# A unit's attention issued in fewer, longer TensorE steps, the state's update as two products of 64 columns, and x's remainder subtracted by VectorE

## The chip, the cores and the metric

The kernel runs on one core of one Trainium2 chip. The metric is the device time of one execution in microseconds (us). The engines are TensorE (PE in the profile; its weight loads have a row of their own, PEld), VectorE (DVE), ScalarE (ACT), GpSimd (POOL) and SyncE (SP), which issues the DMAs. All arithmetic is in 32-bit floats; "fp32" and "fp32r" below are two ways in which TensorE takes them.

## The reference

The program is a complex linear attention followed by a feed-forward layer. For every batch entry b (4) and head h (8) a complex state S of 48 x 48 is carried over 768 positions t; a is first scaled so that its magnitude is at most 0.999:

```
S_t = a_t * S_(t-1) + k_t v_t^T         (complex a_t along k's 48 channels, real k, v)
y_t = q_t^T Re(S_t)
x   = y as (4*768, 8*48) = (3072, 384)
out = gelu(x @ w_in) @ w_out            (384 -> 2048 -> 384)
```

## The kernel before, in words

**Lanes.** The recurrence is made parallel by cutting the 768 positions into chunks: four of 64 positions, then four of 128 (`GROUPS`; two chunks are a group). The running products of a are made on 128 lanes by VectorE, position by position (`scan`, L621), with ScalarE, GpSimd and TensorE helping before and after; k and q are multiplied by the products or their inverses and written to DRAM (`kq`). This is done group by group, lanes 0 to 3.

**Units.** A unit is one batch entry and 128 positions, 24 in all (`unit`, L737). It reads kqn (128 positions x 8 heads x 2 x 96: for each head k's 96 columns, then q's 96, real and imaginary part) and vn (8 heads x 64 columns, of which 48 are v). TensorE then makes, with fp32r transposes, k and q turned (`turn`, L819, four heads at a time); the scores of four heads (`scores`, L831, fp32, 96 rows x 128 columns); `y` (L843, fp32: 128 rows x 64 weight columns, two heads in the two halves of the columns); `y_state` (L849: what comes from the state, 96 rows x 48 columns, two heads side by side in the same way); and for the state's update `add_state` (L801) one fp32 product per head: weights k of 96 columns, moving v of 48. Units 0 to 7 hold two chunks of 64 positions each, units 8 to 23 one chunk of 128; the last chunk of each batch entry (units 20 to 23) needs no update. Between two chunks the state is turned (multiplied by a complex gain): in units 0 to 5 by two TensorE products with 96 weight columns (`turn_by_pe`, L787), from unit 6 on by VectorE or ScalarE and GpSimd (`turn_state`, L775).

**x and its remainder.** The feed-forward layer works with numbers split into an fp32r part (hi) and a remainder (lo). For x = y in PSUM, ScalarE writes hi in two pieces (128 x 128, called x, and 128 x 384, called xT) and sums them for a check of the input's range; TensorE then subtracts hi from y in PSUM with two fp32r products by minus the identity; ScalarE or VectorE copies what is left as lo; six DMAs place one piece (`xT<-x`).

**Blocks.** A block is two or three units' x, 256 or 384 columns (`block`, L913), nine blocks of 2, 3, 3, 3, 3, 3, 3, 2 and 2 units. For each of 16 slices of the middle layer TensorE does nine fp32r products (`first`), ScalarE gelu twice (gh, gf), VectorE or GpSimd gl = gf - gh, and TensorE nine (six) products for the output (`second`). A block needs the x of all of its units before its first product.

**Order.** All of this is written as steps to a list (`Plan`, L109). `either` and `both` leave a step's engine open. `together` makes several TensorE instructions one step, which is issued as a whole when all of its inputs are there. A list scheduler (`forward`, L267) with estimated costs (`FIXED`, `EACH`, `PASS`, `SWITCH`) simulates the engines and takes at each moment the ready step of highest rank; ranks come from the longest way to the end (`natural`) plus a constant for each kind of work (`MORE`). So the instructions' order on each engine is fixed before the run, and each engine works through it in order. A step with at most 64 weight columns in fp32 counts as "narrow", and a change between narrow and not narrow costs `SWITCH` in the estimate.

All instructions issued from the list show line 390 (or 388) in the profile, so they are told apart by their tiles. "att" is a ring of three PSUM banks for units, "ph" and "po" the banks of the blocks.

Of the kernel before, what the change touches and what calls it, by code (L numbers as in the profile page):

```python
# [10 lines left out]
F32 = mybir.dt.float32  # L11
F32R = mybir.dt.float32r
# [65 lines left out]
BYTES = 3.6e5  # L78

ROUND, PASS = 0.462e-3, 0.4219e-3  # L80
SWITCH = 0.09
STAY = 0.0
COLD, WARM = 3.0, 4.0
TABLES = {AF.Ln: "natural_log_exp_and_others", AF.Exp: "natural_log_exp_and_others", AF.Gelu: "gelu"}
NEAR = 0.076
# [5 lines left out]
N_A = 4  # L91
WL = 0.307

MORE = dict(lanes0=-11.06, lanes1=28.05, lanes2=-175.66, lanes3=359.97, weights=-54.39, units=96.75, blocks=41.59)
BIAS = dict(vector=0.49, scalar=-0.32, gpsimd=0.38)


class Step:


    def __init__(self):
        self.options, self.table, self.port = {}, None, set()
        self.before, self.after, self.chain, self.weight = set(), [], None, 1.0
        self.data, self.narrow = 0.0, False


class Plan:
# [16 lines left out]

    @contextmanager
    def together(self):
        self.open = []
        yield
        calls, self.open = self.open, None
        self.add(calls)  # L130
# [27 lines left out]
    def add(self, calls):  # L158
        step = Step()
        n = len(self.steps)  # L160
        engine = calls[0][0]
        cost = 0.08 * (engine == "scalar" and len(calls) > 1)
        for call in calls:
            outs, ins = self.operands(call)
            cost += self.cost(call, outs, ins)
            if engine == "tensor":
                step.narrow = call[1] == "matmul" and call[3]["rhs"].dtype != F32R and call[3]["lhsT"].shape[1] <= 64
            if engine == "sync":
                step.data = max(0.05, math.prod(c for _, c in outs[0].ap) * 4 / BYTES)
            for x in tuple(call[2]) + tuple(call[3].values()):  # L170
                step.table = TABLES.get(x, step.table) if isinstance(x, AF) else step.table
            for x, writes in [(x, False) for x in ins] + [(x, True) for x in outs]:
                self.hold(step, n, x, writes)
        step.options[engine] = calls, cost
        self.ports(step, engine, calls)
        step.before.discard(n)
        step.chain, step.weight = self.chain.get(engine, (None, 1.0))
        step.kind, step.part = self.kind, self.part
        self.steps.append(step)
# [87 lines left out]
    def forward(self, rank):  # L267
# [6 lines left out]
        free = dict.fromkeys(FIXED, 0.0)  # L274
        table = None
        channel = 0.0
        warm, narrow = 0.0, False
        port = dict.fromkeys(FIXED, 0.0)
        other = {"vector": "gpsimd", "gpsimd": "vector"}
        first = lambda some: max(some, key=lambda i: (rank[i], -i))  # L280
# [1 line left out]
        while len(order) < len(steps):  # L282
            best = None
            for e, waiting in pool.items():
                if not waiting:
                    continue
                t = max(free[e], min(ready[i] for i in waiting)) + NEAR
                fits = [i for i in waiting if ready[i] <= t]
                i = first(fits)
                if e == "tensor" and STAY and steps[i].narrow != narrow:  # L290
                    same = [j for j in fits if steps[j].narrow == narrow and rank[j] > rank[i] - STAY]
                    i = first(same) if same else i
                if len(steps[i].options) > 1:
                    ends = {o: max(free[o], ready[i], port[other[o]] if o in steps[i].port else 0.0) + c + BIAS[o] for o, (_, c) in steps[i].options.items()}
                    if ends[e] > min(ends.values()) + 1e-9:
                        fits = [i for i in fits if len(steps[i].options) == 1]
                        if not fits:
                            continue
                        i = first(fits)
                start = max(free[e], ready[i])  # L300
                if e in steps[i].port:
                    start = max(start, port[other[e]])
                if best is None or start < best[0]:
                    best = start, i, e
# [9 lines left out]
            if e == "tensor":  # L314
                if start - free[e] > COLD:
                    warm = start + WARM
                if start < warm:
                    cost *= 2
                cost += SWITCH * (s.narrow != narrow)
                narrow = s.narrow  # L320
            free[e] = end = start + cost
            if e in s.port:
                port[e] = end
# [77 lines left out]
def lanes_and_chunks(ctx, tc, flags, a_lanes, x_lanes, v_units, w_in, w_out, out):  # L401
# [25 lines left out]
    nc.gpsimd.memset(sj, -1.0)  # L427
    nc.gpsimd.affine_select(sj, sj, pattern=[[0, 1]], compare_op=ALU.is_gt, fill=1.0, base=D, channel_multiplier=-1)

    other_half = cst.tile([D2, D2], F32, name="other_half")  # L430
    nc.scalar.mul(other_half[:, 0:D], ident[0:D2, D:D2], -1.0)
    nc.scalar.mul(other_half[:, D:D2], ident[0:D2, 0:D], -1.0)

# [303 lines left out]
    def unit(u):  # L737
# [32 lines left out]
        def bank():  # L770

            p = next(ps_early if early else ps_att)
            return bank() if any(p is x for x in held) else p
# [13 lines left out]
        def turn_by_pe(i, b):  # L787

            sb = st[b]
            m2 = next(m2s)  # L790
            P.vector.tensor_tensor(out=m2.rearrange("p c (h e) -> p c h e", h=H), in0=vap(sb, [[0, 2], [D, H], [1, D]]),
                                   in1=vap(gain[i - 1][:, :, b * H:(b + 1) * H], [[BH, 2], [1, H], [0, D]]), op=ALU.mult)
            p = bank()[0:D2, 0:DM]
            with P.together():
                P.tensor.matmul(out=p, lhsT=ident[0:D2, 0:D2], rhs=m2[:, 0], start=True, stop=False)
                P.tensor.matmul(out=p, lhsT=other_half[:], rhs=m2[:, 1], start=False, stop=True)
            sf = sb.rearrange("p h e -> p (h e)")
            P.either(("scalar", "copy", (sf, p), {}), ("vector", "tensor_copy", (sf, p), {}))
            return p

        def add_state(chunk, turned):  # L801

            i, _, _, t0, size, b = chunk
            sf = st[b].rearrange("p h e -> p (h e)")
            p = bank()[0:D2, 0:DM] if turned is None else turned
            for hh in range(2):
                with P.together():
                    for h in range(hh * 4, hh * 4 + 4):
                        P.tensor.matmul(out=p[:, h * D:(h + 1) * D], lhsT=kn[t0:t0 + size, h], rhs=vn[t0:t0 + size, h, 0:D], start=turned is None, stop=True, skip_group_check=turned is not None)
            if turned is not None:  # L810
                P.either(("scalar", "copy", (sf, p), {}), ("vector", "tensor_copy", (sf, p), {}))
            elif i == 0:
                P.vector.tensor_copy(sf, p)
            else:
                P.vector.tensor_tensor(out=sf, in0=p, in1=sf, op=ALU.add)

        qT, kT, kp, pm = [], [], [], []

        def turn(src, dst, nm, hh):  # L819
            p = next(ps_att)  # L820
            with P.together():
                for j in range(4):
                    P.tensor.transpose(out=p[0:D2, j * 128:(j + 1) * 128].bitcast(F32R), in_=src[:, hh * 4 + j, :].bitcast(F32R), identity=ident_r[:])
            t = next(qTs if nm == "qT" else kps)
            src = p[0:D2, :].rearrange("p (j l) -> p j l", j=4)
            P.either(("scalar", "copy", (t[0:D2], src), {}), ("vector", "tensor_copy", (t[0:D2], src), {}))
            dst.append(t[0:D2])
            if nm == "kT":
                kp.append(t)

        def scores(hh):  # L831
            p = next(ps_att)
# [23 lines left out]
        if early:  # L856
# [4 lines left out]
            held.append(bank())  # L861
            py = held[0].rearrange("p (c l) -> p c l", c=4)
            for hh in range(2):
                turn(kn, kT, "kT", hh)
                turn(qn, qT, "qT", hh)
                scores(hh)
                y(hh)
                for c in with_state:
                    y_state(c, hh)
            for c in with_state:  # L870
                add_state(c, turned[c])
        else:
            for hh in range(2):
                turn(kn, kT, "kT", hh)
                turn(qn, qT, "qT", hh)
                scores(hh)
            held.append(bank())
            py = held[0].rearrange("p (c l) -> p c l", c=4)
            y(0)
            y(1)  # L880
            for c in chunks:
                turned = None
                if c[0]:
                    turned = (turn_by_pe if u < UPE else turn_state)(c[0], c[5])
                    y_state(c, 0)
                    y_state(c, 1)
                if c[0] < NP - 1:
                    add_state(c, turned)
        j = next(j for j in range(len(BLOCKS)) if u < first_unit[j + 1])
        if u == first_unit[j]:  # L890
            xblk[j] = next(xTs)
# [2 lines left out]
        parts = ((py[:, 3], x67[:, 0], x67[:, 1], fc), (py[:, 0:3], xt[:, :, 0], xt[:, :, 1], fc + 1))  # L894
        for at, hi, _, f in parts:
            P.scalar.activation(hi, at, AF.Copy, accum_out=flags[:, f:f + 1])
        with P.together():
            for at, hi, _, _ in parts:
                P.tensor.matmul(out=at, lhsT=minus[:], rhs=hi, start=False, stop=True, skip_group_check=True)
        for at, _, lo, _ in parts:  # L900
            P.either(("scalar", "copy", (lo, at), {}), ("vector", "tensor_copy", (lo, at), {}))

        for c in range(NCC):
            for p0 in (0, 64):
# [317 lines left out]
```

## Time and profile before

| | us |
|---|---|
| median of 3 runs (730.65 to 735.02) | 732.39 |
| the profiled execution's own time | 732.53 |
| its span, first to last instruction | 730.7 |
| PE busy / DVE busy / ACT busy / POOL busy | 672.6 / 452.2 / 457.0 / 72.6 |

A row of a timeline reads: start, duration (both us from the span's start), engine, line, operation, out<-in, shapes, and how many instructions were merged. A matmul's duration holds its way through the array, so successive ones overlap: what one costs is read from the start of one row to the start of the next. An fp32 matmul shows as two records (x8 for four heads). In "128*96 128x48" the first pair is the weights (rows x columns), the second the moving operand. PE's granted clock was 1.00 from 120 us on but for the very end.

### The profile page before, as it was taken

Reading aid. Unit: us, or ns where it says so; the run is one execution under the profiler, and the core shown is the slowest. Engines: PE = TensorE matmul, PEld = TensorE weight load, DVE = VectorE, ACT = ScalarE, POOL = GpSimd, SP = SyncE. Lnnn points to the kernel's source line nnn. Section 1 sums busy time; section 2 is a strip of 40 time slices with the busy share of each in tenths; the row PEclk is TensorE's granted clock in tenths of the full one; section 3 lists DMA queues with packets and bytes.
Section 4 is the critical chain, followed back from the end, with each engine's and each line's share of the span. In section 5 each row is a group of like instructions: output and inputs, shape, how many; then the busy total and the mean of one; then the engine's idle time right before and its main releaser. Section 6 shows DMA issues by size and latency. Waiting matters only on the chain.

```text
span 730.7 us, 12957 instructions
## 1 busy us (share of the span) xinstructions
PE 672.6 (92%) x4742; PEld 607.8 (83%) x4742; DVE 452.2 (62%) x1096; ACT 457.0 (63%) x1082; POOL 72.6 (10%) x95
## 2 busy tenths in 40 slices
PE   4555698998999999999989999999999999999995
PEld 2322487897889999989979899999999999999995
DVE  5999659898999999999978962342233112122121
ACT  8776658899997788888889754433433243253322
POOL 1007211232200000201012000200000000000000
PEclk8865569999999999999999999999999999999998
DMA  9446937679448546666775645212321030010000
GB/s 292 136 118 174 244 90 198 161 197 236 107 101 216 121 113 154 169 161 171 177 200 162 172 104 163 63 34 66 105 74 40 22 97 6 1 38 7 22 2 25
DMA packets 112837, 86.62 MB, mean 119 GB/s; under 512 B 55808, under 2 KB 105088, under 8 KB 112768
## 3 DMA queue, kind: packets, MB, share of 16 engines
q1 hardware_dynamic: 112768, 85.75, 44.5%
q8 instruction: 38, 0.62, 0.4%
q14 instruction: 31, 0.25, 0.1%
HBM read 56.82 MB, written 23.59 MB: 110 GB/s over the span
## 4 chain that ended last, share of the span: by engine, by line
PE 70%; DVE 10%; DMA 8%; ACT 8%; issue 2%; SPq 1%; ACTq 0%; DVEq 0%
PE po L390 26%; PE ph L390 24%; PE att L390 20%; DVE a L390 3%; DMA kqn<-kq 2%; DMA m<-st 2%; DMA kq<-xt 2%; DVE tt L390 2%; ACT tab L390 1%; ACT a L390 1%; DVE xt L390 1%; DVE bt L390 1%; SPq L390 1%; DVE tab L390 1%; ACT L388 1%
## 5 line engine op out<-in xcount | busy, mean ns | idle before, releaser
L390 PE MATMUL ph<-xT,wi_hi 128*128 128x384 f32 (+1 forms) x864 | 210.8, 326 | 2.1 <-DMA xT<-x 2.1
L390 DVE TENSOR_TENSOR gl<-gf,gh 128x384 fp32r<-128x384 f32 (+1 forms) x136 | 70.2, 516 | 160.3 <-ACT gf L390 157.5
L390 PEld LDWEIGHTS ph<-xT,wi_hi 128*128 128x128 f32 x864 | 151.8, 188 | 5.5 <-issue 2.6
L390 ACT ACTIVATE gh<-ph 128x384 fp32r<-128x384 f32 (+1 forms) x144 | 65.6, 456 | 136.0 <-PE ph L390 135.0
L390 PE MATMUL ph<-xT,wi_lo 128*128 128x384 f32 (+1 forms) x432 | 137.0, 317 | 0.0
L390 PE MATMUL po<-wo_hi,gh 128*128 128x384 f32 x384 | 134.3, 350 | 0.3
L390 PE MATMUL po<-wo_lo,gh 128*128 128x384 f32 x384 | 129.7, 338 | 0.0
L390 PE MATMUL po<-wo_hi,gl 128*128 128x384 f32 x384 | 92.9, 343 | 0.2 <-DVE gl L390 0.2
L390 PEld LDWEIGHTS ph<-xT,wi_lo 128*128 128x128 f32 x432 | 81.2, 188 | 0.0
L390 PEld LDWEIGHTS po<-wo_hi,gh 128*128 128x128 f32 x384 | 72.1, 188 | 3.5 <-issue 1.5
L390 PEld LDWEIGHTS po<-wo_lo,gh 128*128 128x128 f32 x384 | 72.4, 188 | 0.0
L390 DVE TENSOR_TENSOR tt<-bt,a 128x192 f32<-128x192 f32 x192 | 69.7, 363 | 1.2
L390 PEld LDWEIGHTS po<-wo_hi,gl 128*128 128x128 f32 x384 | 65.2, 188 | 1.7 <-issue 0.9
L390 ACT ACTIVATE gf<-ph 128x384 f32<-128x384 f32 (+1 forms) x144 | 65.2, 453 | 2.1 <-DVE gl L390 1.9
L390 DVE TENSOR_TENSOR kp<-att,causal 128x512 f32<-128x512 f32 x48 | 33.1, 689 | 38.8 <-PE att L390 32.4
L390 PE MATMUL att<-qT,kp 96*128 96x128 f32 x384 | 54.0, 285 | 0.3 <-DVE kp L390 0.3
L390 PEld LDWEIGHTS att<-qT,kp 96*128 96x128 f32 x384 | 49.9, 197 | 3.1 <-issue 1.3
L390 DVE TENSOR_TENSOR bt<-tt 128x96 f32<-128x96 f32 x192 | 49.5, 258 | 1.4
L390 PE MATMUL po<-wh,ident_r 128*128 128x384 f32 x64 | 34.7, 631 | 13.5 <-DVE wh L390 4.3
L390 PE MATMUL att<-ident_r,kqn 128*96 128x128 f32 x384 | 41.1, 236 | 2.5 <-DMA kqn<-kq 2.1
L390 PEld LDWEIGHTS att<-ident_r,kqn 128*96 128x96 f32 x384 | 36.2, 128 | 7.2 <-issue 2.8
L390 PEld LDWEIGHTS att<-vn,kqn 64*96 64x96 f32 (+1 forms) x384 | 36.1, 163 | 4.7 <-issue 3.3
(176 smaller groups left out, 1057.8 us busy)
## 6 DMA issues: line engine op xcount, KB each, us to landing
kqn<-kq SPq DMA_DIRECT2D x16, 768.0 KB, 5.2
xt<-in_x_lanes_dram SPq DMA_DIRECT2D x24, 384.0 KB, 4.6
kq<-xt SPq DMA_DIRECT2D x24, 384.0 KB, 4.0
kq<-xt SPq DMA_DIRECT2D x48, 192.0 KB, 4.5
a<-in_a_lanes_dram SPq DMA_DIRECT2D x20, 384.0 KB, 3.9
raw<-in_w_pieces_dram SPq DMA_DIRECT2D x16, 384.0 KB, 4.0
raw<-in_moe_w_out_dram SPq DMA_DIRECT2D x16, 384.0 KB, 4.0
vn<-in_v_units_dram SPq DMA_DIRECT2D x24, 256.0 KB, 5.4
```

Source lines behind the costliest of these rows:

```text
L388: self.nc.scalar.preload_act_table_set(table)
L390: getattr(getattr(self.nc, engine), name)(*args, **kw)
```

## The change

Five things are done.

1. **State's update.** `products` takes for each head two products of 64 weight columns instead of one of 96. The weights are columns 0 to 63 and 64 to 127 of kqn's row for that head (k's 96 columns and the first 32 of q's), and they write partitions 0 to 63 and 64 to 127 of the bank; what is made from q is not read. `turn_by_pe` writes all 128 partitions of the bank with zeros in the last 32, for which `other_half` gets 32 columns of zeros.
2. **Longer steps.** In the units from 2 on, y of both halves, the state's part of y and the products of the state's update of a chunk become one step. In all units `turn` takes k's and q's four heads each as one step of eight transposes, into two banks.
3. **x's remainder.** The two products by minus the identity and the copies go; VectorE subtracts hi (in SBUF) from y (in PSUM) in two instructions. The engine is no longer open.
4. **The scheduler's estimates.** TensorE steps have four forms (turn, round, narrow, full), with costs for entering and leaving a form, and a ready step of the same form is taken first where its rank is within `STAY` of the best.
5. **`MORE`** has other constants for each kind of work.

```diff
-SWITCH = 0.09
-STAY = 0.0
+
+ENTER, LEAVE = dict(narrow=0.09), dict(narrow=0.2, turn=0.075)
+STAY = 1.0
...
-MORE = dict(lanes0=-11.06, lanes1=28.05, lanes2=-175.66, lanes3=359.97, weights=-54.39, units=96.75, blocks=41.59)
+MORE = dict(lanes0=34.6, lanes1=-19.14, lanes2=-150.68, lanes3=357.49, weights=-40.2, units=100.95, blocks=82.69)
...
     def together(self):
+        if self.open is not None:
+            yield
+            return
...
-                step.narrow = call[1] == "matmul" and call[3]["rhs"].dtype != F32R and call[3]["lhsT"].shape[1] <= 64
+                step.form = ("turn" if call[1] == "transpose" else "round" if call[3]["rhs"].dtype == F32R else
+                             "narrow" if call[3]["lhsT"].shape[1] <= 64 else "full")
...
-                if e == "tensor" and STAY and steps[i].narrow != narrow:
-                    same = [j for j in fits if steps[j].narrow == narrow and rank[j] > rank[i] - STAY]
+                if e == "tensor" and STAY and steps[i].form != form:
+                    same = [j for j in fits if steps[j].form == form and rank[j] > rank[i] - STAY]
...
-                cost += SWITCH * (s.narrow != narrow)
-                narrow = s.narrow
+                if s.form != form:
+                    cost += ENTER.get(s.form, 0.0) + LEAVE.get(form, 0.0)
+                form = s.form
...
-    other_half = cst.tile([D2, D2], F32, name="other_half")
+    other_half = cst.tile([D2, 128], F32, name="other_half")
+    nc.gpsimd.memset(other_half[:, D2:], 0.0)
...
-            p = bank()[0:D2, 0:DM]
+            whole = bank()[:, 0:DM]
+            p = whole[0:D2]
             with P.together():
-                P.tensor.matmul(out=p, lhsT=ident[0:D2, 0:D2], rhs=m2[:, 0], start=True, stop=False)
-                P.tensor.matmul(out=p, lhsT=other_half[:], rhs=m2[:, 1], start=False, stop=True)
+                P.tensor.matmul(out=whole, lhsT=ident[0:D2, :], rhs=m2[:, 0], start=True, stop=False)
+                P.tensor.matmul(out=whole, lhsT=other_half[:], rhs=m2[:, 1], start=False, stop=True)
             sf = sb.rearrange("p h e -> p (h e)")
             P.either(("scalar", "copy", (sf, p), {}), ("vector", "tensor_copy", (sf, p), {}))
-            return p
-
-        def add_state(chunk, turned):
+            return whole
+
+        def products(chunk, turned):
 
             i, _, _, t0, size, b = chunk
-            sf = st[b].rearrange("p h e -> p (h e)")
-            p = bank()[0:D2, 0:DM] if turned is None else turned
+            p = bank()[:, 0:DM] if turned is None else turned
             for hh in range(2):
                 with P.together():
                     for h in range(hh * 4, hh * 4 + 4):
-                        P.tensor.matmul(out=p[:, h * D:(h + 1) * D], lhsT=kn[t0:t0 + size, h], rhs=vn[t0:t0 + size, h, 0:D], start=turned is None, stop=True, skip_group_check=turned is not None)
+
+                        for c0 in (0, 64):
+                            P.tensor.matmul(out=p[c0:c0 + 64, h * D:(h + 1) * D], lhsT=kqn[t0:t0 + size, h].rearrange("p c d -> p (c d)")[:, c0:c0 + 64],
+                                            rhs=vn[t0:t0 + size, h, 0:D], start=turned is None, stop=True, skip_group_check=turned is not None)
+            return p[0:D2]
+
+        def add_state(chunk, turned, p=None):
+
+            i, _, _, t0, size, b = chunk
+            p = products(chunk, turned) if p is None else p
+            sf = st[b].rearrange("p h e -> p (h e)")
             if turned is not None:
                 P.either(("scalar", "copy", (sf, p), {}), ("vector", "tensor_copy", (sf, p), {}))
             elif i == 0:
...
 
         qT, kT, kp, pm = [], [], [], []
 
-        def turn(src, dst, nm, hh):
-            p = next(ps_att)
+        def turn(hh):
+            sides = [(kn, kT, next(ps_att)), (qn, qT, next(ps_att))]
             with P.together():
-                for j in range(4):
-                    P.tensor.transpose(out=p[0:D2, j * 128:(j + 1) * 128].bitcast(F32R), in_=src[:, hh * 4 + j, :].bitcast(F32R), identity=ident_r[:])
-            t = next(qTs if nm == "qT" else kps)
-            src = p[0:D2, :].rearrange("p (j l) -> p j l", j=4)
-            P.either(("scalar", "copy", (t[0:D2], src), {}), ("vector", "tensor_copy", (t[0:D2], src), {}))
-            dst.append(t[0:D2])
-            if nm == "kT":
-                kp.append(t)
+                for src, _, p in sides:
+                    for j in range(4):
+                        P.tensor.transpose(out=p[0:D2, j * 128:(j + 1) * 128].bitcast(F32R), in_=src[:, hh * 4 + j, :].bitcast(F32R), identity=ident_r[:])
+            for _, dst, p in sides:
+                t = next(qTs if dst is qT else kps)
+                src = p[0:D2, :].rearrange("p (j l) -> p j l", j=4)
+                P.either(("scalar", "copy", (t[0:D2], src), {}), ("vector", "tensor_copy", (t[0:D2], src), {}))
+                dst.append(t[0:D2])
+                if dst is kT:
+                    kp.append(t)
 
         def scores(hh):
             p = next(ps_att)
...
             held.append(bank())
             py = held[0].rearrange("p (c l) -> p c l", c=4)
             for hh in range(2):
-                turn(kn, kT, "kT", hh)
-                turn(qn, qT, "qT", hh)
+                turn(hh)
                 scores(hh)
                 y(hh)
                 for c in with_state:
...
                 add_state(c, turned[c])
         else:
             for hh in range(2):
-                turn(kn, kT, "kT", hh)
-                turn(qn, qT, "qT", hh)
+                turn(hh)
                 scores(hh)
             held.append(bank())
             py = held[0].rearrange("p (c l) -> p c l", c=4)
-            y(0)
-            y(1)
             for c in chunks:
-                turned = None
+                turned = p = None
                 if c[0]:
                     turned = (turn_by_pe if u < UPE else turn_state)(c[0], c[5])
-                    y_state(c, 0)
-                    y_state(c, 1)
-                if c[0] < NP - 1:
-                    add_state(c, turned)
+                with P.together():
+                    if c is chunks[0]:
+                        y(0)
+                        y(1)
+                    if c[0]:
+                        y_state(c, 0)
+                        y_state(c, 1)
+                    if c[0] < NP - 1:
+                        p = products(c, turned)
+                if p is not None:
+                    add_state(c, turned, p)
...
             P.scalar.activation(hi, at, AF.Copy, accum_out=flags[:, f:f + 1])
-        with P.together():
-            for at, hi, _, _ in parts:
-                P.tensor.matmul(out=at, lhsT=minus[:], rhs=hi, start=False, stop=True, skip_group_check=True)
-        for at, _, lo, _ in parts:
-            P.either(("scalar", "copy", (lo, at), {}), ("vector", "tensor_copy", (lo, at), {}))
+        for at, hi, lo, _ in parts:
+            P.vector.tensor_tensor(out=lo, in0=at, in1=hi.bitcast(F32), op=ALU.subtract)
```

More of the change, by code (lines that the diff above doesn't have):

```diff
@@ L103, in __init__ @@
         self.before, self.after, self.chain, self.weight = set(), [], None, 1.0
-        self.data, self.narrow = 0.0, False
+        self.data, self.form = 0.0, None
 class Plan:
@@ L276, in forward @@
         channel = 0.0
-        warm, narrow = 0.0, False
+        warm, form = 0.0, "full"
         port = dict.fromkeys(FIXED, 0.0)
```

## The prediction

> **What bounds the kernel now.** I read the page's span and chain, then the busy times by stage, and then, for the prices, the timeline of TensorE start by start.
>
> ```profile
> span 730.7 us, 12957 instructions
> PE 70%; DVE 10%; DMA 8%; ACT 8%; issue 2%; SPq 1%; ACTq 0%; DVEq 0%
> core 0: us, PE busy (x) PEld busy (x) DVE busy (x) ACT busy (x) POOL busy (x), PEclk, DMA share, GB/s
> 100.00:180.00 80.00, 75.80 (x605) 65.48 (x603) 69.14 (x176) 69.65 (x177) 17.69 (x21) 0.97 0.71 181
> 180.00:440.00 260.00, 256.07 (x1955) 236.20 (x1953) 235.44 (x578) 215.82 (x474) 26.39 (x30) 1.00 0.60 153
> 440.00:724.00 284.00, 283.02 (x2037) 272.77 (x2034) 68.52 (x132) 101.33 (x265) 7.36 (x14) 1.00 0.16 47
> ```
>
> From 180 to 724 us PE is busy 539.1 of 544 us at a granted clock of 1.00. After 440 VectorE has 68.5 of 284 us to do, so TensorE alone bounds there. Between 180 and 440 VectorE is busy for 235.4 of 260 us as well (the lanes), and before 180 PE stands still for the lanes, last here:
>
> ```profile
> 177.51 0.72 PE L390 MATMUL att<-ident_r,kqn 128*96 128x128 f32 x8 [2.12 <-DMA kqn<-kq]
> ```
>
> So I take each microsecond that leaves TensorE's order after about 175 us as a microsecond off the end, and one saved before as nothing. Busy time overstates PE because durations overlap; the prices come from starts. One late unit with an update:
>
> ```profile
> 519.67 0.66 PE L390 MATMUL att<-kp,vn 128*64 128x128 f32 x8
> 520.25 0.88 PE L390 MATMUL att<-vn,kqn 128*96 128x48 f32 x8
> 521.06 0.66 PE L390 MATMUL att<-kp,vn 128*64 128x128 f32 x8
> 521.55 1.04 PE L390 MATMUL att<-qT,st 96*48 96x128 f32 x16
> 522.52 0.88 PE L390 MATMUL att<-vn,kqn 128*96 128x48 f32 x8
> 523.23 0.60 PE L390 MATMUL ph<-xT,wi_hi 128*128 128x384 f32 x2
> 523.67 0.34 PE L390 MATMUL ph<-xT,wi_lo 128*128 128x384 f32 x1
> 523.84 0.22 PE L390 MATMUL att<-x,minus 128*128 128x128 f32 x1
> 523.90 0.39 PE L390 MATMUL att<-xT,minus 128*128 128x384 f32 x1
> 524.13 0.51 PE L390 MATMUL ph<-xT,wi_hi 128*128 128x384 f32 x2
> 524.48 0.34 PE L390 MATMUL ph<-xT,wi_lo 128*128 128x384 f32 x1
> ```
>
> Read from start to start: four heads of the update's products cost 0.71 us (522.52 to 523.23); y of four heads 0.58 where another form follows and 0.49 where y_state does, so leaving costs 0.09; two block products cost 0.35 in peace (524.13 to 524.48) and 0.44 after a unit's work.
>
> **The change part by part, counted from 175 us.**
>
> ```profile
> L390 PE MATMUL att<-vn,kqn 128*96 128x48 f32 x192 | 19.5, 248 | 0.0
> L390 PE MATMUL att<-vn,kqn 64*96 64x48 f32 x128 | 13.4, 249 | 0.0
> L390 PE MATMUL att<-x,minus 128*128 128x128 f32 x20 | 5.0, 250 | 1.4 <-ACT x L390 1.4
> ```
>
> *(a) x's remainder.* The two products cost 0.29 us (523.84 to 524.13), 20 times after 175: 5.8 us off PE. They had lain between block products, with nothing beside them. What VectorE takes over is costed under (e).
>
> *(b) The update's products.* 192 and 128 records are 24 and 16 groups of four heads. Today a group is eight records, 89 ns each (0.71 / 8). The new group is 16 records of 64 columns in column pairs, a form that this trace does not show with 48 moving columns. The nearest rows are y_state of a 64-position chunk, 48 weight columns in pairs with 64 moving columns, and the same product with 64 rows:
>
> ```profile
> 185.59 0.62 PE L390 MATMUL att<-qT,st 96*48 96x64 f32 x16
> 186.14 0.88 PE L390 MATMUL att<-vn,kqn 64*96 64x48 f32 x8
> 186.94 0.91 PE L390 MATMUL po<-wh,ident_r 128*128 128x384 f32 x2
> ```
>
> 16 records of pairs took 0.55 us, or 0.46 without the leaving: 29 ns each. With 128 moving columns they take 55 ns ((0.97 - 0.09) / 16, from 521.55), so a record of a pair goes by its moving length. Bounds for the new record: by the length alone 48/128 of 55, 21 ns, below; above, today's 89 ns for every record, if pairs gain nothing. I take 29, the row with nearly these shapes: 0.46 a group. For 128 rows that saves 0.25 x 24 = 6.0 us. For 64 rows the group costs 0.80 with its entry and leaving (186.14 to 186.94); the new one keeps some change of form inside the merged step, since y uses 128 rows and this 64. That is not shown; between nothing and a full visit of 0.30 (below), I take half, 0.15: 0.80 - 0.46 - 0.15 = 0.19, x 16 = 3.0 us. Together 9.0.
>
> A record's weight load speaks of a limit:
>
> ```profile
> L390 PEld LDWEIGHTS att<-qT,st 96*48 96x48 f32 x416 | 19.4, 123 | 3.1 <-issue 2.3 <-ACT a L390 0.3
> L390 PEld LDWEIGHTS att<-vn,kqn 128*96 128x96 f32 x192 | 18.5, 164 | 1.7 <-issue 1.6
> ```
>
> 96 columns take 41 ns longer to load than 48, or 0.85 ns a column, and 96 columns at that rate are 82 ns, close to the record's 89: today's product is bound by its load, not by its 48 moving columns. If the loads of a pair go one after the other, a record costs 64/96 of 89, 59 ns, and the change loses here (a rival below). Against that stands the 29 ns record of 48 columns: at 0.85 ns a column its load alone is 41 ns, so two loads must overlap.
>
> The Trainium skill has both sides. "TensorE: Matmul & The Clock Gate", Part 3 (The mechanism), says that a weight load overlaps with running products only when the row group differs; here both halves use the same rows, and with the load time that its Part 2 gives (columns / 1.2 ns, 53 ns for 64) a group would be 0.85 us, an estimate by that page, and the time would be near 726. "TensorEngine Tiling (Array Packing)", Key Properties, says that different tiles can load and multiply in parallel. The 29 ns row agrees with the second and not with the first, as far as 48 columns go; no row has 64.
>
> *(c) Fewer visits of the narrow form.* A visit between block products:
>
> ```profile
> 622.59 0.34 PE L390 MATMUL ph<-xT,wi_lo 128*128 128x384 f32 x1
> 622.85 0.66 PE L390 MATMUL att<-kp,vn 128*64 128x128 f32 x8
> 623.44 0.62 PE L390 MATMUL ph<-xT,wi_hi 128*128 128x384 f32 x2
> 623.90 0.34 PE L390 MATMUL ph<-xT,wi_lo 128*128 128x384 f32 x1
> ```
>
> From 622.59 to 623.90 are 1.31 us for one block product (0.175), y (0.49) and two block products (0.35): 0.30 is the visit's price. After 175 us I count 48 unbroken stretches of y and y_state. With the merged step units 8 to 23 need one each and the first units, with two chunks, two: 16 + 10 = 26. The price of those beside an update's product is partly counted in (b), so 0.26 each: 22 x 0.26 = 5.7 us.
>
> *(d) Fewer turns.*
>
> ```profile
> 487.54 0.71 PE L390 MATMUL att<-ident_r,kqn 128*96 128x128 f32 x8
> 488.09 0.59 PE L390 MATMUL ph<-xT,wi_hi 128*128 128x384 f32 x2
> 488.51 0.34 PE L390 MATMUL ph<-xT,wi_lo 128*128 128x384 f32 x1
> ```
>
> The two block products after a turn cost 0.42 instead of 0.35. I count 60 turns followed by block products after 175; at two a unit there will be 40: 20 x 0.07 = 1.4 us. The other side is that k's copy may wait for q's transposes, 0.25 us more per half unit, hidden by block products while a block is in work.
>
> *(e) VectorE's subtraction.*
>
> ```profile
> L390 DVE CAST xT<-att 128x384 fp32r<-128x384 f32 x2 | 1.1, 550 | 0.4 <-PE att L390 0.4
> L390 DVE CAST x<-att 128x128 fp32r<-128x128 f32 x4 | 1.1, 284 | 6.5 <-ACT xT L390 6.5
> ```
>
> The subtraction is not in the trace; the nearest rows are these copies of the same sizes out of PSUM: 0.55 + 0.28 = 0.83 us a unit, 24 units, less the 2.2 us shown: 17.8 us more on VectorE, ScalarE rid of its 42 copies. After 440 the cover is 215 us of idle VectorE. Before, some 11 us come to an engine that has 24.6 us left between 180 and 440; queued behind a subtraction that waits for hi are scan and gl, and for those wait the next lanes and `second`. I cost it at nothing, because TensorE has a reserve there:
>
> ```profile
> 351.64 3.21 SPq L390 DMA_DIRECT2D xT<-x  x5
> 367.55 0.85 ACT L390 COPY raw<-po 128x384 f32<-128x384 f32 x2
> ```
>
> Unit 10, the last of its block, has its x moved at 351.6 to 355 us, while the block before ends near 367: 12 us in hand. If the cover is gone, the price is the rival "lanes" below. The unit's six DMAs on SP (x5 and one more) stay, and are issued no later than now, since a TensorE step drops out ahead of them.
>
> *(f) The rest.* The wider `other_half` has 128 weight columns under 384 moving ones, whose load (at 0.85 ns a column 27 ns more) lies under a longer pass: nothing. The new constants only reorder; that can add or remove waits of a few us, which I put in the range.
>
> Sum: 5.8 + 9.0 + 5.7 + 1.4 = 21.9 us. The profiled execution took 732.53 (span 730.7 and 1.8 around it), the median shown 732.39, so they can be used alike: 732.5 - 21.9 = 710.6.
>
> **The rivals.**
> - *Loads one after the other.* 59 ns a record, 0.94 a group: 24 x (0.71 - 0.94) + 16 x (0.80 - 0.94 - 0.15) = -10.1 in place of +9.0; the sum is 2.8 and the time 729.7. For it: today's product is load-bound. Against: the 29 ns row.
> - *Lanes.* The savings of 175 to 440 only turn into waits for VectorE. After 440 there are 9 remainders (2.6), 10 groups (2.5), 12 visits (3.1) and some turns (0.4): 8.6, and 723.9. For it: VectorE's 91% between 180 and 440. Against: the 12 us reserve.
> - *Pairs gain nothing (the slower side).* In the update's step of each unit the records keep 89 ns whatever their width: 1.42 a group, 24 x -0.71 and 16 x -0.77 = -29.4 against 12.9 from the other parts: 749. It decides from the point where 40 groups eat the other parts' 12.9 us: 0.32 over today's mean of about 0.69 (less the 0.15), about 1.0 a group, 63 ns a record. For it: no row shows 64-column pairs bound by loads. Against: pairs of 48 and 64 columns run at 29 and 55 ns.
> - *Half of it.* The merged step must wait for the turned state and all scores; where no block product is at hand, that gives back part of (c) and (d), and the new order some more: 718 to 722.
>
> **How the numbers follow.** Forecast 0.70 (704 to 717), half 0.08, lanes 0.08, serial loads 0.08, no gain from pairs 0.06. Low end: the 21 ns record gives 5 us more (705), and savings before 175 may count a little: 703. The high end reaches past "lanes" and leaves out the two load rivals (0.14): 727. Within 0.5% (3.7 us) is about what a measurement of this kernel can't tell from no change: serial loads, 0.08, nearly all there; slower 0.06, raised to 0.07 for a bad order. Faster is what is left, 0.85.
>
> **What would show it.** (a) no rows with minus and x, and VectorE rows of 0.55 and 0.28 us. (b) 16 records of kqn and vn at 64 columns in about 0.46 us; 0.94 or 1.4 would name the rival. (c) some 26 narrow stretches after 175, (d) about 40 turns of eight. (e) PE's waits between 180 and 440 no longer than now and the lanes' end near 440. Wrong it would be if a group takes over 1.0 us, or if PE stands idle before 367 us for x of unit 10.

## The result, and the profile after

The kernel after takes 709.67 us (median of 4 runs, 705.37 to 711.52) where the kernel before takes 731.52: a ratio of 0.9685, 95% interval 0.9628 to 0.9742. Run again beside the experiments it gave 707.72 us and 0.9697 (0.9674 to 0.9719); differences below are taken from that ratio, times 731.5. The forecast was 710.6. A few executions below ran in a slower state with a lower granted clock; medians and ratios leave them out.

From the page of the kernel after, the span and the chain of waits, and by stage the busy time (columns as in the prediction's table):

```profile
span 709.7 us, 13839 instructions
PE 62%; DVE 16%; ACT 9%; DMA 9%; issue 3%; SPq 1%; DVEq 0%; ACTq 0%
180.00:440.00 260.00, 253.06 (x2224) 239.58 (x2222) 241.03 (x587) 214.96 (x470) 40.95 (x39) 0.99 0.60 153
440.00:703.00 263.00, 261.70 (x2030) 257.27 (x2029) 72.52 (x146) 92.83 (x246) 4.75 (x12) 1.00 0.17 49
```

TensorE is still the bound after 440 us (261.7 of 263). Between 180 and 440 it is busy 3.0 us less than before, VectorE 5.6 us more (241.0), and VectorE's part of the chain has gone from 10% to 16%. A late unit on TensorE, from the timeline:

```profile
453.71 0.34 PE L396 MATMUL ph<-xT,wi_lo 128*128 128x384 f32 x1
453.98 1.09 PE L396 MATMUL att<-kp,vn 128*64 128x128 f32 x16
454.90 1.04 PE L396 MATMUL att<-qT,st 96*48 96x128 f32 x16
455.78 1.09 PE L396 MATMUL att<-vn,kqn 128*64 128x48 f32 x32
456.80 0.80 PE L396 MATMUL po<-wo_hi,gl 128*128 128x384 f32 x3
```

y of both halves, the state's part and the products now follow each other as one visit, and no row with minus and x is left. The 32 records of the two groups of products take 1.02 us (455.78 to 456.80); less 0.09 for the leaving, that is 29 ns a record and 0.47 a group of four heads, where a group took 0.71. For a chunk of 64 positions:

```profile
185.16 0.62 PE L396 MATMUL att<-qT,st 96*48 96x64 f32 x16
185.71 1.13 PE L396 MATMUL att<-vn,kqn 64*64 64x48 f32 x32
186.78 0.91 PE L396 MATMUL po<-wh,ident_r 128*128 128x384 f32 x2
```

The state's part takes 0.55 as it did where another form followed, so the change from 96 to 64 rows inside the step costs about 0.09, and the products 1.07 instead of 1.02, another 0.05: 0.14 for the step, where the prediction had put half a visit, 0.15, on each group of four heads, that is twice a step.

The subtraction on VectorE, in the groups of instructions:

```profile
L396 DVE TENSOR_TENSOR xT<-att,xT 128x384 fp32r<-128x384 f32 x22 | 12.1, 550 | 9.7 <-ACT x L396 9.5
L396 DVE TENSOR_TENSOR x<-att,x 128x128 fp32r<-128x128 f32 x22 | 6.1, 279 | 0.0
```

0.55 and 0.28 us, the durations of the copies.

**Where the time went.** The first turn of unit 4 marks the place from which the prediction counted:

```profile
174.42 0.73 PE L396 MATMUL att<-ident_r,kqn 128*96 128x128 f32 x8 [3.88 <-DMA kqn<-kq]
```

It stood at 177.51 before. From there to the span's end were 553.2 us (730.7 - 177.51) and are 535.3: 17.9 us saved, and 3.1 ahead of it, together the 21.0 by which the spans differ. So the stretch gave 4.0 us less than the sum of 21.9, and the 3.1 had been counted as nothing. The split is that of one execution: in the profile of the repeated kernel the turn stands at 172.26 and the span is 704.9, so 20.6 us were saved in the stretch and 5.3 ahead of it. TensorE's waits inside the stretch, after and then before:

```profile
PE po L396 <- DVE gl L396: 2.4, 1, 2.4
PE att L396 <- DVE x L396: 1.3, 2, 1.1
PE att L396 <- ACT qT L396: 0.8, 1, 0.8
PE att L396 <- DVE kp L396: 0.8, 2, 0.5
PE ph L396 <- ACT gf L396: 0.8, 1, 0.8
PE att L396 <- ACT kp L396: 0.4, 1, 0.4
PE po L396 <- ACT gh L396: 0.2, 1, 0.2
```

```profile
PE att L390 <- ACT x L390: 1.8, 2, 1.4
PE att L390 <- DVE kp L390: 1.1, 2, 0.8
PE att L390 <- ACT gf L390: 0.7, 1, 0.7
PE po L390 <- DVE gl L390: 0.2, 1, 0.2
```

They rose from 3.8 to 6.7 us, by 2.9, most of it waits for VectorE (6.0 in the repeated profile). The granted clock fell as well; in the kernel before it was 1.00 from the first turn to the last product. Two windows of the kernel after, one behind the 3.88 us wait shown above, one behind the 2.4 us wait for gl (the granted clock stands third from the end), and a block product in the second:

```profile
175.00:179.00 4.00, 4.00 (x23) 4.00 (x22) 3.33 (x9) 2.25 (x6) 0.00 (x0) 0.57 0.99 223
380.00:384.00 4.00, 4.00 (x17) 4.00 (x16) 3.77 (x11) 2.61 (x11) 0.00 (x0) 0.59 0.64 140
381.32 0.53 PE L396 MATMUL po<-wo_hi,gh 128*128 128x384 f32 x1
381.64 0.53 PE L396 MATMUL po<-wo_lo,gh 128*128 128x384 f32 x1
```

For 3.4 us each time the granted clock was 0.50 and a block product cost 0.32 us instead of 0.175, so each time lost some 1.5 us (an estimate from these numbers). The repeated profile has one such time in the stretch. So TensorE's own work became shorter by 17.9 + 2.9 + 3.0 = 23.8 us in the one profile and by 20.6 + 2.2 + 1.5 = 24.3 in the other: the sum of 21.9 was some 2 us too small for the work, and the added waits and the lost clock took 4 to 6 us that it did not have.

The reserve of 12 us in which unit 10's x used to be ready has gone; from the timelines of SyncE and VectorE:

```profile
348.94 3.69 SPq L396 DMA_DIRECT2D xT<-x  x6
```

```profile
354.19 1.01 DVE L396 COPY raw<-po 128x384 f32<-128x384 f32 x2
```

The six DMAs are issued until 352.6 and the block ahead of it is copied out from 354.2: some 2 us, where the transfers of x between 345 and 365 us took 1.8 to 5.4 us from issue to landing. Up to here 10.3 us have been saved (179.8 us from the first turn of unit 4 to this copy, 190.0 before). In the kernel after, the chain of work that ended last has no TensorE row between 262 and 379.5 us, where it comes back through the wait for gl; before, it was on TensorE from 322 to 357. So there the lanes and the engines that serve them now set the time.

### The profile page after: what moved, and what is told of

Same layout as the page of the kernel before. It is cut to its first block, busy times and chain, and to the rows that moved or that the text cites. A ratio compares the mean times of both kernels' runs of the same rounds, so it can differ in the third digit from the quotient of the medians.

```text
span 709.7 us, 13839 instructions
## 1 busy us (share of the span) xinstructions
PE 647.6 (91%) x5142; PEld 595.9 (84%) x5142; DVE 465.5 (66%) x1126; ACT 447.6 (63%) x1062; POOL 82.3 (12%) x100
## 4 chain that ended last, share of the span: by engine, by line
PE 62%; DVE 16%; ACT 9%; DMA 9%; issue 3%; SPq 1%; DVEq 0%; ACTq 0%
PE po L396 24%; PE ph L396 22%; PE att L396 16%; DVE a L396 4%; DMA kqn<-kq 2%; DVE tt L396 2%; DVE xt L396 2%; DMA m<-st 2%; ACT tab L396 2%; DVE bt L396 2%; DMA kq<-xt 2%; SPq L396 1%; ACT a L396 1%; DVE tab L396 1%; DVE wh L396 1%
## 5 line engine op out<-in xcount | busy, mean ns | idle before, releaser
L396 PEld LDWEIGHTS ph<-xT,wi_hi 128*128 128x128 f32 x864 | 154.5, 190 | 2.2 <-ACT gf L396 1.4
L396 DVE TENSOR_TENSOR bt<-tt 128x96 f32<-128x96 f32 x192 | 51.0, 266 | 1.1
L396 ACT COPY kp<-att 96x512 f32<-96x512 f32 x45 | 26.2, 583 | 26.9 <-PE att L396 26.8
L396 PE MATMUL att<-ident_r,kqn 128*96 128x128 f32 x384 | 36.4, 239 | 5.6 <-DMA kqn<-kq 3.9
L396 PEld LDWEIGHTS att<-ident_r,kqn 128*96 128x96 f32 x384 | 32.3, 127 | 8.7 <-issue 4.5
```

The costliest lines, as they stand in the source:

```text
L396: getattr(getattr(self.nc, engine), name)(*args, **kw)
```

## The experiments

**The width of the products.** One product of 96 columns a head again, all else as after.

```diff
-                        for c0 in (0, 64):
-                            P.tensor.matmul(out=p[c0:c0 + 64, h * D:(h + 1) * D], lhsT=kqn[t0:t0 + size, h].rearrange("p c d -> p (c d)")[:, c0:c0 + 64],
+                        P.tensor.matmul(out=p[0:D2, h * D:(h + 1) * D], lhsT=kn[t0:t0 + size, h],
```

> The kernel after, with the state's update back at one product of 96 weight columns a head. Theory (a pair of 64-column products costs 29 ns a record, today's single one 89): 40 groups of four heads after 175 us cost 9.0 us more, so about 719 beside 709.7 for the kernel after, and a group of eight records takes 0.7 us again. Rival (the gain came from the longer steps and the new order, not from the width): 710 to 712.

Measured 723.45 us, ratio 0.9891 (0.9856 to 0.9926), 14.2 +- 3.0 us over the kernel after. A late unit:

```profile
485.34 1.04 PE L396 MATMUL att<-qT,st 96*48 96x128 f32 x16
486.32 1.56 PE L396 MATMUL att<-vn,kqn 128*96 128x48 f32 x16
487.70 0.77 PE L396 MATMUL po<-wo_hi,gl 128*128 128x384 f32 x3
```

The two groups take 1.38 us and y_state 0.98 again, against 1.02 and 0.88: 0.46 us a unit, 5.5 in twelve; the chunks of 64 positions cost 0.42 more each in this trace, 3.4 in eight. So TensorE's share is 8.9 us, the 9.0 of the theory. Some 5 us more came with the re-planned order; where they went is not shown. The rival fell.

**What the pair does.** The same products, neighbours in the same half of the array; the order of the steps is unchanged.

```diff
-                    for h in range(hh * 4, hh * 4 + 4):
-                        for c0 in (0, 64):
+                    for c0 in (0, 64):
+                        for h in range(hh * 4, hh * 4 + 4):
```

> The kernel after, with the same 64-column products in another order inside the step: for four heads first all of columns 0 to 63, then all of columns 64 to 127, so that neighbours share the half of the array. The order of steps is unchanged. Theory (two loads overlap only where neighbours lie in different halves): a record goes from 29 ns to 59 (64/96 of 89), a group of 16 records from 0.46 to 0.94 us, 40 groups after 175 us 19 us more, about 729. Rival (64 columns are cheap by themselves, pairing is not what helps): 710. Second rival (a record keeps 89 ns without a partner, whatever its width): 1.42 a group, 748.

Measured 712.99 us, ratio 0.9732 (0.9698 to 0.9766), 2.6 +- 3.0 us over the kernel after.

```profile
455.95 1.44 PE L396 MATMUL att<-vn,kqn 128*64 128x48 f32 x32
457.31 0.80 PE L396 MATMUL po<-wo_hi,gl 128*128 128x384 f32 x3
```

32 records take 1.36 us, less 0.09 is 40 ns a record on the mean: neither 29 nor 59 nor 89. A group costs 0.64 in this order, hardly less than the single 96-column product's 0.69 (1.38 / 2). At 0.34 us a unit's chunk, 20 chunks after 175 us, TensorE's own price is 6.8 us; the ratio shows less, its interval ends at 5.6. The weight loads at the end of the step, the last five of one half:

```profile
456.89 0.37 PEld L396 LDWEIGHTS att<-vn,kqn 128*64 128x64 f32 x5
```

A load lasts 0.14 us, so the five start within 0.23 us: 58 ns apart, the 59 of the theory. The mean is lower because the halves still overlap where the order goes from one to the other: 32 records at 58 ns would take 1.87 us and not 1.27, so each of the three changes saves some 0.2 us (an estimate). The run does not take the partner away altogether. Where it is away, the theory's price holds; its 729 us fell because the overlap stays for part of the step.

**What sets the 40 and the 29 ns.** Each product in two pieces of 24 moving columns; units of even number in the order by halves, units of odd number in pairs.

```diff
+                    order = [(h, c0) for h in range(hh * 4, hh * 4 + 4) for c0 in (0, 64)]
+                    if u % 2 == 0:
+                        order.sort(key=lambda x: x[1])
+                    for h, c0 in order:
+                        for e in (0, 24):
```

> The kernel after, with each 64-column product of the state's update made in two pieces of 24 moving columns, and in units of even number first one half's columns for four heads, then the other's. What is computed is the same. It asks what sets the 41 ns of a record without a partner and the 29 ns of one with. If the moving length sets it: 20 ns without a partner, and with one 10 to 15, unless a floor stops it. If the load of 64 columns sets it: 41 and 29 again.

A single run, 770.89 us. A unit in pairs, then one by halves:

```profile
459.28 2.05 PE L396 MATMUL att<-vn,kqn 128*64 128x24 f32 x64
461.26 0.61 PE L396 MATMUL ph<-xT,wi_hi 128*128 128x384 f32 x2
...
482.39 3.24 PE L396 MATMUL att<-vn,kqn 128*64 128x24 f32 x64
485.56 0.61 PE L396 MATMUL ph<-xT,wi_hi 128*128 128x384 f32 x2
```

1.98 and 3.17 us for 64 records, less 0.09: 30 and 48 ns on the mean. Half the moving length did not make a record shorter. The weight loads from a part of each of these two steps, then of a step in the kernel after (pairs, 48 moving columns) and in the width run:

```profile
459.39 0.72 PEld L396 LDWEIGHTS att<-vn,kqn 128*64 128x64 f32 x22
482.45 0.72 PEld L396 LDWEIGHTS att<-vn,kqn 128*64 128x64 f32 x11
455.78 0.73 PEld L396 LDWEIGHTS att<-vn,kqn 128*64 128x64 f32 x22
486.40 0.93 PEld L396 LDWEIGHTS att<-vn,kqn 128*96 128x96 f32 x10
```

In the same 0.72 us 22 loads start in pairs and 11 in one half. Less the 0.14 of the last load, these are ten steps of 58 ns, with two loads in a step or one, and at 48 moving columns the step is the same. So each half takes one load every 58 ns whether the other half works or not, and the pair's 29 ns is half of that; 40 and 48 are means of 58 and of the overlaps at the changes of half. Loads of 96 columns come every 85 ns ((0.93 - 0.164) / 9, by the 164 ns that one such load lasts). 58 for 64 columns and 85 for 96 are 0.9 ns a column, so the load sets the pace, and not the moving columns or a fixed cost of each record.

**x's remainder back on TensorE.**

```diff
-        for at, hi, lo, _ in parts:
-            P.vector.tensor_tensor(out=lo, in0=at, in1=hi.bitcast(F32), op=ALU.subtract)
+        with P.together():
+            for at, hi, _, _ in parts:
+                P.tensor.matmul(out=at, lhsT=minus[:], rhs=hi, start=False, stop=True, skip_group_check=True)
+        for at, _, lo, _ in parts:
+            P.either(("scalar", "copy", (lo, at), {}), ("vector", "tensor_copy", (lo, at), {}))
```

> The kernel after, with x's remainder taken by two TensorE products and copied by ScalarE or VectorE as before. Theory (TensorE sets the end, VectorE has room): 20 pairs of 0.29 us after 175 us, so 5.8 us more, about 715.5. Rival (VectorE's lanes set the end between 180 and 440 us, and the subtraction's 11 us there were paid): only the nine pairs after 440 count, 2.6 us, less what the lanes win back: 708 to 712.

Measured 714.94 us, ratio 0.9787 (0.9739 to 0.9836): 6.6 +- 3.9 us over the kernel after. The theory's 5.8 holds; the rival's upper end, 712, lies just below the interval, which begins at 712.4. The reverse, the same edit made in the kernel before and nothing else:

> The kernel before, with only x's remainder changed: VectorE's two subtractions in place of TensorE's two products and the copies. Theory (20 pairs of 0.29 us after 175 us leave TensorE): 5.8 us less, about 726, give or take the 4 to 7 us of a re-planned order. Rival (VectorE, busy for 235 of 260 us between 180 and 440, pays for it): 730 to 738.

Measured 721.86 us, ratio 0.9869 (0.9850 to 0.9889), 9.6 us under the kernel before. VectorE does not pay for it; the rival fell. The gain is larger than the 5.8 us of the two products: in this trace the first turn of unit 4 stands at 171.94 and the span is 720.2, so 4.9 us were saved behind the turn and 5.6 ahead of it, where the theory had counted nothing.

**VectorE's reserve.** Both subtractions done twice.

```diff
         for at, hi, lo, _ in parts:
-            P.vector.tensor_tensor(out=lo, in0=at, in1=hi.bitcast(F32), op=ALU.subtract)
+            for _ in range(2):
+                P.vector.tensor_tensor(out=lo, in0=at, in1=hi.bitcast(F32), op=ALU.subtract)
```

> The kernel after, with VectorE's two subtractions of each unit done twice, so that VectorE has 20 us more to do, 11 of them before 440 us, where it is busy for 241 of 260 us. Theory (VectorE has a reserve, TensorE sets the end): 709 to 712. Rival (VectorE's lanes set the pace between 180 and 440 us, so that its work is paid in full there): 11 us more, about 721.

Measured 711.70 us, ratio 0.9745 (0.9722 to 0.9769): 3.5 +- 2.4 us over the kernel after, for 20 us more on VectorE. It is not paid in full, and not free: about a sixth of it. The rival fell. Five units' subtractions, 4.1 us, lie in the stretch from 262 to 379.5 us in which the chain is off TensorE; that these are what is paid would fit, but is not shown.

**The longer steps.** y, y_state and the products as steps of their own.

```diff
-                with P.together():
-                    if c is chunks[0]:
-                        y(0)
-                        y(1)
...
-                if p is not None:
-                    add_state(c, turned, p)
+                if c[0] < NP - 1:
+                    add_state(c, turned)
```

> The kernel after, with y of each half, y_state of each half and the two halves of the update's products as steps of their own again. Theory (each visit of the narrow form costs 0.26 to 0.30 us): the stretches after 175 us rise from 24 towards 40 or 50, 4 to 7 us more, 714 to 717. Rival (the scheduler keeps equal forms together anyway, or the long step's waits give the gain back): 708 to 711.

Measured 717.05 us, ratio 0.9796 (0.9769 to 0.9824): 7.2 +- 2.6 us. In time order I count 49 narrow stretches after 174 us where the kernel after has 24: 25 at 0.26 to 0.30 are 6.5 to 7.5 us. The trace agrees in part: its first turn of unit 4 comes later, at 179.38, and the 536.7 us from there hold 4.5 us of waits and one time at half clock; without these TensorE's work is some 5 us longer than in the two profiles of the kernel after. The theory holds, at the low end of the count.

**The turns.** k's and q's transposes as two steps.

```diff
-            with P.together():
-                for src, _, p in sides:
+            for src, _, p in sides:
+                with P.together():
```

> The kernel after, with k's and q's transposes of four heads as two steps again. Theory (a turn costs the block products behind it 0.07 us): up to 40 stretches of eight after 175 us become up to 80 of four; if all part, 2.8 us more, and if the scheduler keeps half together, 1.4 us: 711 to 712.5. Rival (a step of eight makes k's copy wait, and the new waits before turns come from that): 707 to 709, less than now.

Measured 716.71 us, ratio 0.9809 (0.9783 to 0.9834): 8.2 +- 2.5 us. Neither theory nor rival. The turns lie in 52 stretches instead of 40, which at 0.07 us are 0.8 us. The rest is not that price; what it is, this run alone does not show.

**The order alone.** The scheduler's part of the change in the kernel before; the old constants of `MORE` in the kernel after; and one constant of the kernel after moved a little.

> The kernel before, with only the scheduler's part of the change: four forms with their costs of entering and leaving, STAY of 1.0, and the new constants. The work of each engine is that of before. Theory (the order alone moves little; the gain is in the work that left TensorE): 728 to 733. Rival (the order itself saves most of the visits and turns, 7 us): 722 to 726. Second rival (the constants were fitted to the new work and don't suit the old): 734 to 740.

Measured 732.15 us, ratio 1.0016 (0.9983 to 1.0050): the new forms and constants together bring the old work nothing.

```diff
-MORE = dict(lanes0=34.6, lanes1=-19.14, lanes2=-150.68, lanes3=357.49, weights=-40.2, units=100.95, blocks=82.69)
+MORE = dict(lanes0=-11.06, lanes1=28.05, lanes2=-175.66, lanes3=359.97, weights=-54.39, units=96.75, blocks=41.59)
```

> The kernel after, with the constants for each kind of work (MORE) of the kernel before. Every product and copy is that of the kernel after; only the order differs. Theory (the gain is work that left TensorE; a re-planned order costs what the other re-planned runs cost over their share of TensorE, some 4 to 7 us): 711 to 715. Rival (the order does not matter, and 9 us for parting the turns is the turns' own price): 706 to 709. Second rival (the constants hold a large part of the gain): 718 or more.

Measured 717.47 us, ratio 0.9816 (0.9797 to 0.9835): 8.7 +- 2.1 us over the kernel after, with every product and copy the same: above the theory's range, near the second rival's 718. So an order that does not suit the work costs as much as parting the turns did.

```diff
-units=100.95
+units=103.95
```

> The kernel after, with one constant of MORE moved a little (units from 100.95 to 103.95), which gives the units' steps a slightly higher rank. The same work in another order. Theory (an order found by the scheduler for other constants than the fitted ones is some us worse by chance): 710 to 714. Rival (orders that differ little cost the same): 706 to 709.

Measured 708.94 us, ratio 0.9721 (0.9683 to 0.9759): 1.8 +- 3.2 us. A small move changes the order in many places and costs little or nothing; the theory's 2 to 7 us is not shown.

Several of the re-planned profiles show a wait at the place named above. The block of units 8 to 10 begins with a wait for x, here in the width run and in the nudged one:

```profile
362.12 0.59 PE L396 MATMUL ph<-xT,wi_hi 128*128 128x384 f32 x2 [1.55 <-DMA xT<-x]
```

```profile
353.09 0.59 PE L396 MATMUL ph<-xT,wi_hi 128*128 128x384 f32 x2 [1.24 <-DMA xT<-x]
```

In the kernel after there is no such wait. These are 1 to 2 us and don't make up 8, and the nudged kernel, which has one, is hardly slower. Where the rest of the 8.7 us of the old constants goes stays open: the profiled execution took 709.80 us, the shortest of that kernel's six, so its trace does not show what the median shows. A part goes with the clock: the shortest execution had a mean granted clock of 0.949, the other five (715.8 to 719.0 us) 0.937 to 0.944. One more time at half clock, 3.4 us, lowers the mean over 710 us by 0.0024, so 0.012 are some five of them, or 7.5 us, an estimate. The turns' run goes the same way (713.6 us at 0.952, 719.8 at 0.939); the repeated kernel after does not show it (0.945 to 0.955, 706.8 to 711.0 us). What let the clock fall in these executions, no trace shows. The forms and `STAY` were not undone by themselves in the kernel after.

## Why the prediction was right, point by point

The direction and the size were right, 710.6 against 709.7, and TensorE's work is what paid, but the closeness is luck: TensorE's work became some 24 us shorter where the sum said 21.9, waits and clock inside the stretch took back some 6, and 3.1 were won ahead of it, where nothing had been counted. The bound held after 379.5 us; ahead of that the lanes took part in it.

- **(a) x's remainder, 5.8 us:** right. The rows vanished, the copies' durations were the subtraction's, and putting it back cost 6.6 +- 3.9.
- **(b) the products, 9.0 us:** right in size. The row taken for the price, 29 ns for a pair's record, was the measured one, 0.47 a group against 0.46, and undoing it costs TensorE 8.9. That the two halves work at the same time on the same rows is shown (22 loads against 11 in 0.72 us), which agrees with "TensorEngine Tiling (Array Packing)", Key Properties, of the Trainium skill and not with the rule on row groups in "TensorE: Matmul & The Clock Gate", Part 3 (The mechanism). The prediction's 0.85 ns a column and the 59 ns of its rival "loads one after the other" were right as prices of one half (58 measured); that rival fell because the halves overlap, even in part of the order by halves. The rival "pairs gain nothing" had the price wrong: a record of 64 columns takes 58 ns in its half and not 89. That the row gave exactly 29 was luck: by the prediction's own rows it goes by its moving length (29 at 64 columns, 55 at 128), while the new record goes by its load, 58 / 2. Too large was the change of form in a chunk of 64 positions, 0.30 a step against 0.14: 1.3 us in eight chunks, a part of what the sum missed.
- **(c) fewer visits, 5.7 us:** right. 24 stretches (26 foreseen) of 48; parting them again costs 7.2 +- 2.6, some 5 of it seen as TensorE's work in the trace.
- **(d) fewer turns, 1.4 us:** the count was right, 40 stretches, but TensorE now waits there for VectorE and ScalarE: at turns the 1.3 us of "att" for x and the 0.4 for ACT's kp, and at the scores behind a turn the 0.8 for qT, where one wait of 0.4 us stood at a turn before. In the trace nothing of (d) is seen to be left.
- **(e) VectorE at nothing:** a little too low. Twenty microseconds more cost 3.5 +- 2.4, and the 12 us reserve named as its cover is used up; that TensorE's becoming faster did this as much as VectorE's load is not shown. One of the prediction's signs of being wrong, TensorE idle before 367 us for unit 10's x, did come, though small (0.9 us in the repeated profile): VectorE's subtraction for unit 10 ends at 348.9, and the second half of a turn starts only then.

```profile
348.94 0.48 PE L396 MATMUL att<-ident_r,kqn 128*96 128x128 f32 x4 [1.07 <-DVE x L396]
```

  The rival "lanes" did not come true as a whole, but in part, as the chain between 262 and 379.5 us shows: TensorE's waits for VectorE rose there.
- **(f) the order, "waits of a few us":** this term was the worst sized. The constants alone are worth 8.7 +- 2.1 us in the kernel after; with the new forms they are worth nothing in the kernel before. They were costed at nothing and put in the range; with the old ones the time would have been 717.5, the upper end of the forecast's own range. The four undone parts together cost 36.2 us (14.2 + 6.6 + 7.2 + 8.2) where the whole change brought 22.2; that fits each undone part's also getting an order that was not fitted to it.

## What to carry to other kernels

Where one engine's order is full, the price of an instruction is the time from its start to the next one's start, read from the timeline in the place where it stands; durations and busy shares would not have given 0.71, 0.30 or 0.29. When the order comes from a scheduler whose constants were fitted, one part taken out re-plans everything: a difference of 5 to 9 us in 710 is then no proof of that part's worth, and the trace must show the price on the engine, as it did for the products, or the run with the constants alone must stand beside it. A mean over a group can also hide its price: 40 and 48 ns were the same 58 with different shares of overlap, which the single loads showed. And before counting a saving in full, look for what feeds the engine next: here a reserve of 12 us ahead of one block was nearly used up.

## What the runs showed of the hardware

A record of an fp32 product with 96 weight columns and 48 moving ones took 85 to 89 ns; its loads came 85 ns apart. With 64 weight columns the loads of one half of the array's columns came 58 ns apart, at 48 and at 24 moving columns, and the other half kept the same pace beside it, so that a record of a pair took 29 to 30 ns. Shortening the moving operand from 48 to 24 columns gained nothing at 64 weight columns. A change of the number of rows (96 to 64) inside a run of column pairs cost 0.09 us, about what leaving the form costs. After waits of 3.88 us (174.42) and 2.39 us (379.50) in the kernel after, and of 2.58 us (172.26) in its repeated profile, the granted clock was 0.50 for 3.4 us; after 2.12 us (177.51) in the kernel before and 2.52 us (376.44) in the repeated profile it stayed at 1.00. So waits of nearly the same length did or did not cost clock.
